# Gated linear attention with a gated convolution block: q, k and f packed into 12 of 16 columns, and one more convolution on VectorE

## The chip, the core and the metric

The kernel runs on one core of a Trainium2 chip. The metric is the device time of one execution in microseconds (us). The engines are named as in the profile: PE is TensorE's matmul (PEld its weight loads), DVE is VectorE, ACT is ScalarE, POOL is GpSimd, and SP is SyncE, whose queue issues nearly all transfers.

## The reference

```python
# B, H, S, D = 4, 8, 768, 48; five taps; d_model = H * D = 384; everything float32
f = 1 / (1 + exp(-f_logit))
for t in range(S):                                   # per batch and head, a 48 x 48 state
    state = f[t][:, None] * state + outer(k[t], v[t])
    y[t] = q[t] @ state
x = y.transpose(0, 2, 1, 3).reshape(B, S, H * D)
gate = sigmoid(sum(conv_w[j] * xp[:, j:j+S] for j in range(5)))  # xp: x with 4 zeros ahead, per channel
out = ((gate * (x @ w_val)) @ w_out)
```

## The kernel before

**Layout.** The sequence is cut into six chunks c of 128 positions (C). Two heads share a column: head 0 lies in rows 0 to 47, head 1 in rows 64 to 111, and rows 48 to 63 and 112 to 127 are pad rows. A column is a pair (batch b, pair of heads p), so there are BP = 16 columns of 128 positions, batch 3 being columns 12 to 15. q, k and v have two buffers each (`qb`, `kb`, `vb`), the decay logarithms three (`E1`, named e), beside `E2` (also e).

**Attention of a chunk.** `loadf`, `loadk`, `loadq`, `loadv` bring the operands in spans of columns. `pexp` and `pln` (ACT) make the decay logarithms. Their prefix sum over time is a matmul with the triangle `tri` for chunks 0 and 1 (`cum`, into PSUM banks `bk`) and a scan on DVE for chunks 2 to 5 (`scan`). `exp2` and `exp1` (ACT) take the exponentials with both signs, `pmulk` and `pmulq` (DVE) multiply them onto k and q in place. Per batch, `scores` or, from chunk 2, `scoresq` (PE, into `aps`), `mask` (DVE, into `asb`), `ktrans` (PE) and `kevac` (ACT), `dstate` (PE), `apply` or, for two batches at once, `applyq` (PE), `cross` and `crossb` (PE: q against the running state `ss`), and `xevac` (ACT, into `xf`). `stadd` (DVE) and `stmul` (ACT, eight pieces for one half of the columns) advance the state; `stmul` scales by the last column of `E1`.

**Projection.** The units n are 0 and 1 (chunk 0, two batches each), 2 to 5 (chunks 1 to 4), 6 and 7 (chunk 5, two batches each). `msplit` and `mlow` split x in a high and a low part. The convolution is either `conv n j` (PE, tap weights `wd`, five taps over three groups m of 128 channels: 60 matmuls for a chunk) for chunks below `CS`, or `mlast n m` (ACT) with four `mtap n m j` (DVE, in place in `gt`, for chunk 5 in `re`) from chunk `CS` on. Then `gate` (ACT), `mval` (PE, nine matmuls for each m), `mmul` (DVE), `mhigh` (ACT), `mrest` (DVE), `mout` (PE, nine matmuls), `mstore` (ACT and a transfer). `halo` hands the last four positions to the next chunk. In chunks below `CS` the channels lie rotated by 32-row groups (`TURN`), so that `wturn` makes rotated weights for the later chunks and one halo goes by transfers.

**Order.** `PROGRAM` is a text that lists every piece; each engine, and SP's queue, executes its instructions in just this order (class `Ordered`, line 129, is why nearly every row of the profile carries L129). What a piece waits for is kept by semaphores. `general` is a fallback that runs only when a flag at the end says that the fast way lost range.

Of the kernel before, what the change touches and what calls it, by code (L numbers as in the profile page):

```python
# [57 lines left out]
loadk 1 0; weight 0; loadq 1 0; scores 0 0; kevac 0 0; pmulk 0 2; loadf 2 0; exp1 0 2; dstate 0 0; mask 0 0;  # L58
exp2 0 1; ktrans 0 2; loadv 1 0; ktrans 0 3; exp1 0 1; pmulk 0 1; kevac 0 2; apply 0 0; weight 0; pexp 1 1; okc 0;
pmulq 0 1; ktrans 0 1; pmulq 0 2; xevac 0 0; scores 0 1; pln 1 1; weight 0; weight 0; weight 0; weight 0;  # L60
kevac 0 1; taps; cum 1 1; loadq 2 0; kevac 0 3; pexp 1 0; loadk 2 0; mask 0 1; pln 1 0; dstate 0 1; scores 0 2;
exp2 1 1; stadd 0 0; cum 1 0; exp1 1 1; mask 0 2; weight 2; weight 2; weight 2; apply 0 1; exp2 1 0;
weight 2; scores 0 3; weight 2; loadv 2 0; xevac 0 1; msplit 0; weight 2; dstate 0 2; loadq 2 1; exp1 1 0;
mask 0 3; weight 1; dstate 0 3; loadk 2 1; apply 0 2; weight 2; stadd 0 1; apply 0 3; weight 1; pmulk 1 0;
xevac 0 2; loadf 3 0; xevac 0 3; weight 1; ktrans 1 1; msplit 1; conv 0 0; weight 1; kevac 1 1; weight 1;
conv 0 1; pmulq 1 0; loadv 2 1; conv 0 2; pmulk 1 1; cross 1 0; pexp 2 0; weight 1; scores 1 0; okc 1; halo 1;
mlow 1; ktrans 1 0; conv 0 3; mask 1 0; weight 2; pln 2 0; conv 0 4; pmulq 1 1; scores 1 1; kevac 1 0; gate 0 2;
scan 2 0; dstate 1 1; loadk 3 0; dstate 1 0; apply 1 0; gate 0 0; mask 1 1; weight 4; gate 0 1; cross 1 1;
weight 1; ktrans 1 3; stadd 1 0; weight 4; wturn 0; scores 1 2; mlow 0; exp2 2 0; weight 4; apply 1 1;
weight 4; crossb 1 0; mask 1 2; weight 1; loadv 3 0; kevac 1 3; exp1 2 0; ktrans 1 2; loadq 3 0; pmulk 2 0;  # L70
dstate 1 3; scores 1 3; stmul 1 0; weight 4; apply 1 2; kevac 1 2; loadk 3 1; mask 1 3; weight 3; xevac 1 0;
pexp 3 0; dstate 1 2; wturn 1; weight 4; mval 0 2; stadd 1 1; scan 2 1; mval 1 1; weight 4; weight 3; mval 1 0;
pln 3 0; apply 1 3; mmul 0 2; weight 3; exp2 2 1; mval 0 1; weight 3; loadv 3 1; mmul 1 0; weight 3; exp1 2 1;
mval 0 0; weight 3; xevac 1 1; crossb 1 1; mmul 0 1; weight 3; pmulk 2 1; mval 1 2; xevac 1 2; loadq 3 1;
stmul 1 1; mmul 1 1; scan 3 1; ktrans 2 3; ktrans 2 2; kevac 2 3; ktrans 2 1; loadf 4 0; kevac 2 2; ktrans 2 0;
kevac 2 1; dstate 2 3; kevac 2 0; dstate 2 2; mmul 1 2; xevac 1 3; dstate 2 0; mmul 0 0; exp2 3 1; halo 2;
dstate 2 1; stadd 2 1; conv 2 0; pmulq 2 0; exp1 3 1; conv 2 1; stadd 2 0; msplit 2; scan 3 0; scoresq 2 1;
cross 2 0; pexp 4 0; conv 2 2; mask 2 1; weight 3; conv 2 3; exp2 3 0; mlow 2; scoresq 2 0; exp1 3 0; conv 2 4;
loadk 4 0; pln 4 0; mask 2 0; weight 4; mval 2 1; okc 3; pmulk 3 0; mhigh 1 0; mhigh 0 0; mhigh 0 2; mrest 1 0;
applyq 2 0; mhigh 1 2; mrest 0 2; mhigh 1 1; mrest 1 2; mhigh 0 1; mrest 1 1; gate 2 2; scan 4 1; loadq 4 0;  # L80
xevac 2 1; mout 1 1; loadv 4 0; stmul 2 0; mrest 0 1; mrest 0 0; mout 1 0; pmulq 2 1; mstore 1 1; gate 2 1; mout 0 2;
xevac 2 0; okc 2; pmulq 3 0; mstore 1 0; gate 2 0; scoresq 2 2; mstore 0 2; mmul 2 1; cross 2 1; pmulq 3 1; mout 0 1;
mask 2 2; mout 1 2; mstore 0 1; scan 4 0; scoresq 2 3; mstore 1 2; mout 0 0; loadk 4 1; mask 2 3; exp2 4 0; mval 2 0;
pmulk 3 1; exp2 4 1; scoresq 3 3; pmulk 4 0; applyq 2 1; mstore 0 0; mmul 2 0; exp1 4 1; pmulk 4 1; exp1 4 0;
ktrans 4 1; mhigh 2 1; okc 4; pmulq 4 0; loadv 4 1; stmul 2 1; loadq 4 1; ktrans 3 2; ktrans 4 0; mask 3 3;
xevac 2 3; ktrans 4 2; loadf 5 0; xevac 2 2; mval 2 2; mrest 2 1; mhigh 2 0; halo 3; kevac 3 2; mrest 2 0; mlast 3 1;
mlast 3 0; mtap 3 1 0; scoresq 3 0; msplit 3; mmul 2 2; dstate 3 2; mtap 3 0 0; ktrans 3 1; ktrans 3 3; kevac 4 2;
mask 3 0; ktrans 3 0; kevac 3 1; kevac 3 3; dstate 4 2; mtap 3 0 1; kevac 3 0; dstate 3 1; mhigh 2 2; dstate 3 3;
mtap 3 0 2; dstate 3 0; kevac 4 1; scoresq 3 1; stadd 3 1; pexp 5 0; mrest 2 2; ktrans 4 3; mtap 3 0 3; loadk 5 0;
mout 2 1; mask 3 1; kevac 4 3; mlast 3 2; mlow 3; kevac 4 0; pln 5 0; mout 2 2; mtap 3 2 0; mtap 3 2 1; gate 3 0;  # L90
mval 3 0; mtap 3 2 2; mtap 3 2 3; mstore 2 2; scan 5 1; gate 3 2; mout 2 0; mstore 2 1; mmul 3 0; exp2 5 1;
scoresq 4 1; scan 5 0; dstate 4 3; dstate 4 0; cross 3 0; exp1 5 1; applyq 3 0; stadd 3 0; mtap 3 1 1; exp2 5 0;
mtap 3 1 2; exp1 5 0; mtap 3 1 3; mval 3 2; loadq 5 0; mask 4 1; xevac 3 0; loadv 5 0; gate 3 1; pmulk 5 0;
scoresq 3 2; mmul 3 2; xevac 3 1; dstate 4 1; okc 5; mhigh 3 0; check; loadk 5 1; mval 3 1; mstore 2 0; mrest 3 0;
stmul 3 0; mask 3 2; mhigh 3 2; stadd 4 0; scoresq 4 0; mmul 3 1; cross 3 1; mrest 3 2; mhigh 3 1; applyq 3 1;
mask 4 0; mrest 3 1; pmulk 5 1; mout 3 2; xevac 3 3; loadv 5 1; pmulq 4 1; xevac 3 2; loadq 5 1; mlast 4 2; halo 4;
mlast 4 1; pmulq 5 0; mout 3 1; mlast 4 0; mtap 4 1 0; stmul 3 1; mtap 4 0 0; msplit 4; mtap 4 0 1; mout 3 0;
pmulq 5 1; mstore 3 1; mstore 3 2; mlow 4; scoresq 5 0; cross 4 0; mstore 3 0; stadd 4 1; applyq 4 0; mtap 4 1 1;
mtap 4 1 2; mtap 4 1 3; mval 4 0; stmul 4 0; mask 5 0; mtap 4 2 0; xevac 4 0; gate 4 1; mtap 4 2 1; cross 5 0;
xevac 4 1; mtap 4 2 2; scoresq 4 3; mtap 4 2 3; mval 4 2; mask 4 3; gate 4 2; mtap 4 0 2; mtap 4 0 3; scoresq 4 2;  # L100
mmul 4 2; gate 4 0; count; mval 4 1; mask 4 2; mhigh 4 2; mmul 4 0; mrest 4 2; mhigh 4 0; scoresq 5 3; mmul 4 1;
cross 4 1; mrest 4 0; mhigh 4 1; applyq 4 1; mrest 4 1; mout 4 1; stmul 4 1; mask 5 3; xevac 4 2; xevac 4 3;
mout 4 2; mlast 5 2; halo 5; msplit 5; mtap 5 2 0; mtap 5 2 1; mlast 5 1; cross 5 1; mlow 5; scoresq 5 2; mstore 4 1;
mlast 5 0; mout 4 0; mstore 4 2; mask 5 2; mtap 5 2 2; mtap 5 1 0; applyq 5 1; mstore 4 0; mtap 5 1 1; mtap 5 2 3;
mtap 5 1 2; gate 5 2; mval 5 1; mtap 5 1 3; xevac 5 2; xevac 5 3; mtap 5 0 0; gate 5 1; mlast 7 2; mtap 5 0 1;
msplit 7; mval 5 0; mtap 5 0 2; mlast 7 1; mmul 5 1; mlast 7 0; mtap 7 1 0; mhigh 5 1; mlow 7; mval 5 2; mtap 5 0 3;
mrest 5 1; gate 5 0; mtap 7 2 0; mval 7 0; mmul 5 0; mmul 5 2; mhigh 5 0; mval 7 2; mtap 7 2 1; mhigh 5 2; mrest 5 0;
scoresq 5 1; mrest 5 2; mval 7 1; mtap 7 2 2; mask 5 1; mout 5 2; mtap 7 2 3; mtap 7 0 0; gate 7 2; mtap 7 0 1;
mmul 7 2; mtap 7 0 2; mhigh 7 2; applyq 5 0; mtap 7 0 3; mstore 5 2; mrest 7 2; mtap 7 1 1; gate 7 0; mtap 7 1 2;
mmul 7 0; mtap 7 1 3; mhigh 7 0; mout 5 1; gate 7 1; mrest 7 0; xevac 5 1; mmul 7 1; xevac 5 0; mlast 6 2; mlast 6 1;  # L110
mtap 6 2 0; mlast 6 0; mtap 6 1 0; mout 5 0; mhigh 7 1; mtap 6 0 0; msplit 6; mtap 6 1 1; mrest 7 1; mstore 5 1;
mlow 6; mout 7 0; mtap 6 1 2; mstore 5 0; mtap 6 0 1; mval 6 2; mtap 6 0 2; mstore 7 0; mtap 6 0 3; mtap 6 1 3;
# [797 lines left out]
```

## Time and profile before

| | |
|---|---|
| median of 3 runs | 194.43 us (192.79 to 195.23) |
| profiled execution | 193.15 us |
| span of its profile | 191.5 us |
| granted TensorE clock | 0.995 |
| bytes moved | 32.64 MB, mean 170 GB/s |

The span is the time from the first to the last instruction; the profiled execution's own time is 1.65 us longer. In the rows, "out<-in" names the tiles, "x" counts instructions, "busy, mean ns" are the time that a group covers and the length of one instruction. Matmuls overlap, so the sum of their lengths is more than the time that they cover. A float32 matmul has two records.

### The profile page before, as it was taken

To read this page: it belongs to the slowest core of one execution; us is meant where nothing else is said; L and a number is where in the kernel's file an instruction comes from. 1 tells how busy PE (TensorE), PEld (TensorE's weight loads), DVE (VectorE), ACT (ScalarE), POOL (GpSimd) and SP (SyncE) were. 2 spreads that over 40 slices of the span, in tenths; PEclk is the share of its full clock that TensorE was granted. 3 is DMA by queue.
4 is the path that set the end of the run, shared out by engine and by line. 5 is a ranking of instruction groups with operands and counts; after the bars stand their busy time and mean duration, and the time that the engine had idled before them with its cause. 6 is when DMAs were issued, how large, how long until landed. Compare 5 with 4: busy or idle time off the path is not lost.

```text
span 191.5 us, 8303 instructions
## 1 busy us (share of the span) xinstructions
PE 180.2 (94%) x3706; PEld 144.8 (76%) x3706; DVE 162.2 (85%) x233; ACT 144.8 (76%) x284; POOL 13.7 (7%) x42
## 2 busy tenths in 40 slices
...
GB/s 194 344 419 416 416 415 409 415 349 245 203 114 285 41 113 62 206 128 135 350 48 104 113 12 266 130 183 156 15 3 3 3 167 3 3 54 4 140 87 65
DMA packets 12522, 32.64 MB, mean 170 GB/s; under 512 B 3008, under 2 KB 5440, under 8 KB 11456
## 3 DMA queue, kind: packets, MB, share of 16 engines
...
q10 hardware_dynamic: 432, 0.39, 0.7%
...
## 4 chain that ended last, share of the span: by engine, by line
PE 56%; DVE 19%; ACT 13%; issue 6%; DMA 3%; POOL 0%; ACTq 0%; DVEq 0%
PE bk L129 49%; PE aps L129 8%; DVE re L129 7%; DVE gt L129 5%; ACT ss L129 4%; DMA out<-osb 3%; ACT e L129 2%; ACT xf L129 2%; DVE asb L129 2%; DVE qb L129 1%; DVE rg L129 1%; DVE xL L129 1%; ACT osb L129 1%; DVE rqb L129 1%; ACT re L129 1%
## 5 line engine op out<-in xcount | busy, mean ns | idle before, releaser
L129 ACT ACTIVATE e<-e 112x512 f32<-112x512 f32 (+4 forms) x38 | 36.6, 997 | 4.1 <-DMA e<-in_ft 2.0
L129 PE MATMUL bk<-rg,woH 128*128 128x512 f32 (+1 forms) x108 | 30.1, 365 | 0.1
L129 DVE TENSOR_TENSOR asb<-aps,tri 128x768 f32<-128x768 f32 (+1 forms) x24 | 24.9, 1039 | 5.4 <-PE aps L129 4.0
L129 DVE SCALAR_TENSOR_TENSOR gt<-xf,cws,gt 128x512 f32<-128x512 f32 x36 | 26.5, 748 | 1.5 <-ACT gt L129 0.9
L129 PEld LDWEIGHTS aps<-qb,kb 48*64 48x64 f32 (+1 forms) x640 | 19.9, 144 | 7.3 <-issue 4.8
L129 PE MATMUL bk<-asb,vb 128*32 128x64 f32 (+2 forms) x1280 | 24.4, 232 | 0.4 <-issue 0.4
L129 PE MATMUL aps<-qb,kb 48*64 48x128 f32 (+2 forms) x640 | 23.7, 257 | 0.1
L129 PEld LDWEIGHTS bk<-asb,vb 128*32 128x32 f32 (+1 forms) x1280 | 20.0, 108 | 4.1 <-issue 1.1
L129 PEld LDWEIGHTS bk<-rg,woH 128*128 128x128 f32 x108 | 18.6, 188 | 4.3 <-issue 0.8
L129 DVE TENSOR_TENSOR kb<-kb,e 112x1024 f32<-112x1024 f32 (+1 forms) x13 | 14.8, 1137 | 6.0 <-DMA kb<-in_k 3.5
L129 PE MATMUL bk<-rg,woL 128*128 128x512 f32 (+1 forms) x54 | 19.4, 358 | 0.0
L129 ACT ACTIVATE ss<-u,e 112x48 f32<-112x48 f32 x64 | 15.3, 324 | 3.9 <-PE bk L129 3.9
L129 DVE TENSOR_TENSOR_SCAN e<-keep,e 112x1024 f32<-112x1024 bf16 x8 | 18.3, 2282 | 0.0
L129 PE MATMUL bk<-qb,ss 48*32 48x128 f32 x640 | 15.8, 275 | 1.5 <-ACT cb L129 1.2
L129 ACT COPY osb<-bk 128x512 f32<-128x512 f32 (+1 forms) x20 | 9.8, 495 | 9.1 <-DMA out<-osb 7.3
L129 DVE TENSOR_TENSOR qb<-qb,e 112x1024 f32<-112x1024 f32 (+1 forms) x13 | 14.8, 1146 | 0.0
L129 ACT COPY xf<-bk 128x384 f32<-128x384 f32 x24 | 10.8, 473 | 4.6 <-PE bk L129 4.6
L129 PEld LDWEIGHTS bk<-qb,ss 48*32 48x32 f32 x640 | 10.6, 106 | 4.6 <-issue 1.4
L129 PE MATMUL bk<-xH,wvH 128*128 128x256 f32 (+1 forms) x36 | 13.3, 370 | 0.4 <-ACT xf L129 0.4
L129 PE MATMUL bk<-xL,wvH 128*128 128x256 f32 (+1 forms) x36 | 12.2, 339 | 0.0
L129 PE MATMUL bk<-xH,wvL 128*128 128x256 f32 (+1 forms) x36 | 12.1, 337 | 0.0
L129 ACT CAST rg<-gt 128x512 fp32r<-128x512 f32 (+1 forms) x18 | 9.3, 546 | 3.7 <-DVE gt L129 3.7
...
## 6 DMA issues: line engine op xcount, KB each, us to landing
...
```

Of the source, the lines that this page charges most:

```text
L129: ins = emit(*a, **kw)
```

## The change

From chunk `DF = 1` on q, k and f hold 12 columns: batch 3's 48 rows of a head are laid out by the host in the pad rows of batches 0, 1 and 2 (16 rows each). `pexp`, `pln`, `cum`, `scan`, `exp1`, `exp2`, `pmulk` and `pmulq` then work on 128 rows and 12 columns, in spans of 8 and 4. After the multiplication new pieces `mvk`, `mvq` copy batch 3's rows by transfers on SP's queue into columns 12 to 15 (four transfers for the first span, two for the second), and `mve` does so for the last position of `E1` (six transfers), which `stmul` reads. `CS` goes from 2 to 1: chunk 1's convolution is done by `mlast` and `mtap`, its channels lie unrotated, its projection uses the rotated weights, and the halo by transfers is that of chunk 1. The order is written anew. The three tiles' unused rows are set once on POOL.

```diff
-CS = 2
+CS = 1
+DF = 1
+BD = BP - NP
+dense = lambda c, spans: [(a, min(b, BD)) for a, b in spans] if c >= DF else spans
+high = lambda c: 128 if c >= DF else 112
...
+    nc.gpsimd.memset(okc, 1.0)
...
+    for c in range(max(DF, 1), NB):
+        nc.gpsimd.memset(kw[c][32:64, BD:], 0.0)
+    for c in range(max(DF, 1), NE):
+        nc.gpsimd.memset(E1[c][32:64, BD + (2 if c == 2 else 0) :, C - 1 : C], 0.0)
...
     def scan(c, x0, x1):
-        fl = lambda t: t[:112, x0:x1].rearrange("p a t -> p (a t)")
+        fl = lambda t: t[: high(c), x0:x1].rearrange("p a t -> p (a t)")
...
     def pmul(t, e, c, x0, x1):
-        t = t[c % NB]
-        DVE.tensor_tensor(out=t[:, x0:x1], in0=t[:, x0:x1], in1=e[:112, x0:x1], op=ALU.mult)
+        t = t[c % NB][: high(c)]
+        DVE.tensor_tensor(out=t[:, x0:x1], in0=t[:, x0:x1], in1=e[: high(c), x0:x1], op=ALU.mult)
+    def move(t, x0, x1, cols=slice(0, C)):
+        for b in range(x0 // NP, x1 // NP):
+            for s in range(2):
+                SP.dma_start(t[s * 64 + 16 * b : s * 64 + 16 * b + 16, BD:, cols],
+                             t[s * 64 + D : s * 64 + 64, b * NP : (b + 1) * NP, cols])
...
+        "mvk": lambda c, n: move(kw[c % NB], *spans["s"](c)[n]), "mvq": lambda c, n: move(qw[c % NB], *spans["s"](c)[n]),
+        "mve": lambda c: move(E1[c % NE], 0, BD, slice(C - 1, C)),
...
     (host layout)
+        for b in range(B - 1):
+            for s in range(2):
+                y[DF:, s * 64 + D : s * 64 + 64, b * NP : (b + 1) * NP] = y[DF:, s * 64 + 16 * b : s * 64 + 16 * b + 16, BD:]
```

`PROGRAM` goes from 631 pieces to 665: five `conv 2 j` are gone, and three `mlast`, twelve `mtap`, ten `mvk`, ten `mvq` and four `mve` are new. Its start, and the stretch with the first moves of chunk 2:

```diff
-halo 0; loadf 0 0; loadf 0 1; loadq 0 0; loadv 0 0; loadk 0 0; loadk 0 1; loadk 0 2; wload 0; loadf 1 1; pexp 0 0;
-loadv 0 1; pln 0 0; busy 6; cum 0 0; loadq 0 1; pexp 0 2; loadq 0 2; loadf 1 0; pln 0 2; wload 1; exp2 0 0; busy 2;
-cum 0 2; exp1 0 0; pmulk 0 0; pexp 0 1; wload 2; pmulq 0 0; loadv 0 2; pln 0 1; ktrans 0 0; exp2 0 2; cum 0 1;
+halo 0; loadf 0 0; loadk 0 0; loadf 0 1; loadq 0 2; loadq 0 0; loadk 0 1; loadv 0 2; loadf 1 1; loadq 0 1; pexp 0 0;
+wload 0; pln 0 0; busy 6; cum 0 0; loadv 0 0; exp2 0 0; exp1 0 0; loadf 1 0; pmulk 0 0; pexp 0 1; loadv 0 1; busy 2;
+ktrans 0 0; pln 0 1; loadk 0 2; pexp 0 2; cum 0 1; pmulq 0 0; kevac 0 0; wload 2; pln 0 2; scores 0 0; wload 1;
+exp2 0 1; loadv 1 0; cum 0 2; exp1 0 1; loadk 1 0; pmulk 0 1; loadq 1 0; pexp 1 1; mask 0 0; pln 1 1; weight 0;
...
+mval 1 0; mvk 2 0; xevac 1 3; mval 1 1; weight 3; exp2 3 0; wturn 1; weight 3; scoresq 2 1; stmul 1 1;
+weight 3; mval 1 2; loadv 3 1; weight 3; mmul 0 1; mask 2 1; mval 0 2; weight 4; weight 3; loadf 4 0; mve 2;
+exp1 3 0; mmul 1 2; applyq 2 0; halo 2; mmul 0 2; msplit 2; okc 2; scan 3 1; mmul 1 1; exp2 3 1; mlow 2; scoresq 2 2;
+exp1 3 1; mvq 2 0; xevac 2 1; ktrans 2 1; xevac 2 0; ktrans 2 0; pmulq 3 1; kevac 2 1; mval 2 0; mve 3; mask 2 2;
+weight 3; pexp 4 0; mmul 1 0; pmulq 3 0; mhigh 1 2; dstate 2 1; mhigh 1 1; mvq 3 1; mhigh 0 0; scoresq 2 3;
...
```

More of the change, by code (lines that the diff above doesn't have):

```diff
@@ L58 @@
[L58 to L112, printed above, removed]
@@ new lines @@
+ktrans 0 0; pln 0 1; loadk 0 2; pexp 0 2; cum 0 1; pmulq 0 0; kevac 0 0; wload 2; pln 0 2; scores 0 0; wload 1;
+exp2 0 1; loadv 1 0; cum 0 2; exp1 0 1; loadk 1 0; pmulk 0 1; loadq 1 0; pexp 1 1; mask 0 0; pln 1 1; weight 0;
+ktrans 0 1; weight 0; pmulq 0 1; exp2 0 2; loadf 2 0; cum 1 1; weight 0; weight 0; weight 0; weight 0;
+taps; scores 0 1; kevac 0 1; pexp 1 0; dstate 0 1; mask 0 1; loadq 2 0; pln 1 0; dstate 0 0; loadk 2 0; apply 0 0;
+exp1 0 2; pmulk 0 2; apply 0 1; xevac 0 0; okc 0; stadd 0 0; ktrans 0 2; exp2 1 1; loadv 2 0; pmulq 0 2; cum 1 0;
@@ new lines @@
+xevac 0 1; kevac 0 2; msplit 0; exp1 1 1; mlow 0; scores 0 2; exp2 1 0; ktrans 0 3; mask 0 2; loadk 2 1; exp1 1 0;
+dstate 0 2; kevac 0 3; scores 0 3; okc 1; loadq 2 1; dstate 0 3; mask 0 3; weight 2; apply 0 2; weight 2;
+stadd 0 1; apply 0 3; xevac 0 2; weight 2; loadf 3 0; weight 2; xevac 0 3; msplit 1; pmulk 1 0; conv 0 0;
+loadv 2 1; pmulk 1 1; conv 0 1; mlow 1; ktrans 1 1; pmulq 1 0; ktrans 1 0; kevac 1 1; conv 0 2; kevac 1 0; mvk 1 1;
+weight 2; pexp 2 0; scores 1 0; weight 2; pmulq 1 1; cross 1 0; weight 2; mask 1 0; weight 1; dstate 1 1;
@@ new lines @@
+pln 2 0; mvq 1 1; dstate 1 0; conv 0 3; stadd 1 0; weight 1; scan 2 0; scores 1 1; apply 1 0; weight 1;
+ktrans 1 2; exp2 2 0; conv 0 4; weight 1; mvk 1 0; kevac 1 2; weight 1; exp1 2 0; dstate 1 2; weight 1;
+mvq 1 0; gate 0 1; mask 1 1; weight 2; scores 1 2; scan 2 1; halo 1; gate 0 0; apply 1 1; gate 0 2;
+pmulq 2 0; weight 1; crossb 1 0; loadk 3 0; exp2 2 1; mask 1 2; weight 4; loadv 3 0; cross 1 1; loadk 3 1;
+ktrans 1 3; loadq 3 0; pmulk 2 0; scores 1 3; wturn 0; stmul 1 0; pmulk 2 1; apply 1 2; mask 1 3; weight 1;
@@ new lines @@
+mvk 2 1; weight 4; scoresq 2 0; xevac 1 0; weight 4; xevac 1 1; cross 2 0; exp1 2 1; weight 4; kevac 1 3;
+apply 1 3; weight 4; pexp 3 0; pmulq 2 1; mval 0 0; weight 4; mvq 2 1; pln 3 0; mask 2 0; weight 3; mve 1;
+dstate 1 3; crossb 1 1; mmul 0 0; weight 3; stadd 1 1; mval 0 1; scan 3 0; xevac 1 2; weight 4; loadq 3 1;
+mval 1 0; mvk 2 0; xevac 1 3; mval 1 1; weight 3; exp2 3 0; wturn 1; weight 3; scoresq 2 1; stmul 1 1;
+weight 3; mval 1 2; loadv 3 1; weight 3; mmul 0 1; mask 2 1; mval 0 2; weight 4; weight 3; loadf 4 0; mve 2;
@@ new lines @@
+applyq 2 1; mtap 2 0 0; mlast 2 2; mvk 3 0; stadd 2 0; mtap 2 2 0; stmul 2 0; loadv 4 0; mtap 2 1 0; mout 0 2;
+mtap 2 0 1; loadq 4 1; xevac 2 3; mtap 2 0 2; xevac 2 2; mout 0 1; mstore 0 2; mtap 2 0 3; mtap 2 1 1; mout 1 0;
+gate 2 0; mtap 2 1 2; mout 1 2; mtap 2 1 3; mstore 0 1; mout 0 0; mmul 2 0; mstore 1 0; gate 2 1; mtap 2 2 1;
+mstore 1 2; scoresq 3 0; mmul 2 1; mstore 0 0; mout 1 1; mtap 2 2 2; mtap 2 2 3; mval 2 2; mstore 1 1; mask 3 0;
+gate 2 2; mhigh 2 1; halo 3; scan 4 0; mhigh 2 0; ktrans 3 0; msplit 3; ktrans 3 1; scoresq 3 1; mmul 2 2;
@@ new lines @@
+ktrans 2 3; kevac 3 0; loadk 5 0; mask 3 1; ktrans 2 2; kevac 3 1; dstate 3 0; kevac 2 3; loadk 4 1; kevac 2 2;
+mlow 3; dstate 3 1; mhigh 2 2; dstate 2 3; dstate 2 2; exp2 4 0; cross 3 0; loadv 4 1; mrest 2 2; mval 3 0;
+mrest 2 0; mrest 2 1; mlast 3 0; stadd 2 1; mlast 3 2; stadd 3 0; mout 2 1; mtap 3 0 0; stmul 2 1; pmulk 4 0;
+mout 2 0; mtap 3 0 1; exp1 4 0; mvk 4 0; mtap 3 0 2; mstore 2 1; mtap 3 0 3; mlast 3 1; loadf 5 0; mout 2 2;
+pmulq 4 0; mstore 2 0; gate 3 0; mtap 3 1 0; mvq 4 0; mtap 3 1 1; scoresq 4 1; mstore 2 2; mtap 3 1 2; applyq 3 0;
@@ new lines @@
+mmul 3 0; pexp 5 0; mtap 3 1 3; pmulk 3 1; mtap 3 2 0; mval 3 2; mvk 3 1; mask 4 1; loadq 5 0; gate 3 1; loadv 5 0;
+mtap 3 2 1; scoresq 3 2; mtap 3 2 2; xevac 3 1; mtap 3 2 3; ktrans 3 2; xevac 3 0; ktrans 3 3; stmul 3 0; mask 3 2;
+loadk 5 1; mval 3 1; scan 4 1; gate 3 2; okc 3; kevac 3 3; cross 4 0; mmul 3 2; kevac 3 2; dstate 3 3; mhigh 3 0;
+mmul 3 1; dstate 3 2; mhigh 3 2; mrest 3 0; scoresq 3 3; mhigh 3 1; stadd 3 1; cross 3 1; exp2 4 1; mrest 3 1;
+ktrans 4 0; mask 3 3; ktrans 4 1; scoresq 4 0; mrest 3 2; kevac 4 1; pmulk 4 1; kevac 4 0; dstate 4 1; exp1 4 1;
@@ new lines @@
+mask 4 0; dstate 4 0; mvk 4 1; pln 5 0; applyq 3 1; mve 4; stadd 4 0; pmulq 4 1; scan 5 0; mvq 4 1; mout 3 1;
+xevac 3 2; xevac 3 3; loadq 5 1; msplit 4; loadv 5 1; scan 5 1; scoresq 4 2; halo 4; okc 4; exp2 5 0; mlow 4;
+mout 3 0; exp1 5 0; mask 4 2; mstore 3 1; mlast 4 2; pmulq 5 0; mval 4 1; stmul 3 1; mtap 4 2 0; mvq 5 0; mtap 4 2 1;
+scoresq 4 3; mlast 4 0; mtap 4 2 2; mlast 4 1; cross 4 1; mtap 4 2 3; mstore 3 0; applyq 4 0; mtap 4 1 0; exp2 5 1;
+mtap 4 1 1; exp1 5 1; gate 4 2; mask 4 3; mval 4 2; okc 5; mtap 4 1 2; xevac 4 1; pmulq 5 1; xevac 4 0; check;
@@ new lines @@
+mvq 5 1; stmul 4 0; mval 4 0; mmul 4 2; pmulk 5 1; mtap 4 0 0; mvk 5 1; applyq 4 1; mtap 4 1 3; mtap 4 0 1; gate 4 1;
+mtap 4 0 2; mmul 4 1; ktrans 4 3; mtap 4 0 3; xevac 4 3; ktrans 4 2; xevac 4 2; count; cross 5 0; pmulk 5 0;
+kevac 4 3; kevac 4 2; scoresq 5 2; gate 4 0; halo 5; mvk 5 0; msplit 5; dstate 4 2; mmul 4 0; dstate 4 3; mask 5 2;
+mout 3 2; mlow 5; scoresq 5 0; stadd 4 1; mstore 3 2; mval 5 1; mhigh 4 1; mask 5 0; mhigh 4 2; mhigh 4 0; mrest 4 1;
+stmul 4 1; mrest 4 0; scoresq 5 1; mrest 4 2; mval 5 0; mask 5 1; mlast 5 2; mlast 5 1; mtap 5 2 0; mlast 5 0;
```

75 lines of the change are left out of this document (49 added, 26 removed).

## The prediction

> **What bounds the kernel now.** I read the page's busy line first, then busy time by stage, then the chain of work that ended last, and last the order of instructions on TensorE and VectorE.
>
> ```profile
> PE 180.2 (94%) x3706; PEld 144.8 (76%) x3706; DVE 162.2 (85%) x233; ACT 144.8 (76%) x284; POOL 13.7 (7%) x42
> ```
>
> ```profile
> 0.00:14.00 14.00, 11.03 (x84) 8.69 (x84) 7.38 (x17) 10.42 (x20) 3.45 (x16) 1.00 0.88 315
> 14.00:184.00 170.00, 166.28 (x3600) 133.35 (x3600) 154.86 (x218) 133.21 (x262) 10.29 (x26) 1.00 0.46 162
> 184.00:191.50 7.50, 2.92 (x25) 2.72 (x23) 0.00 (x0) 1.12 (x3) 0.00 (x0) 0.88 0.32 97
> ```
>
> The columns of the stages are PE, PEld, DVE, ACT and POOL busy, the granted clock (1.00, so no throttle to win back), the DMA share and GB/s. From 14 to 184 us PE has 3.7 us without work in 170, DVE 15.1. PE leads, DVE is second.
>
> ```profile
> 120.33 9.49 PE bk L129 x212
> 155.50 2.09 DVE gt L129 x3
> 168.19 0.80 DVE re L129 x2
> 183.58 3.35 PE bk L129 x26
> ```
>
> ```profile
> 159.67 0.40 PE L129 MATMUL bk<-xL,wvH 128*128 128x512 f32 x1
> 159.91 0.39 PE L129 MATMUL bk<-xH,wvL 128*128 128x512 f32 x1
> 160.14 0.40 PE L129 MATMUL bk<-xH,wvHt 128*128 128x512 f32 x1
> ```
>
> The chain (start, length, what) runs on PE up to about 150 us and then mostly on DVE, and returns to PE at 183.58. But the matmuls beside that DVE stretch start 0.24 us apart without a hole, each counted as about 0.40 because it overlaps the next. So both engines are full there: whatever shortens PE helps only as far as DVE finishes earlier too. That is the main doubt of this prediction.
>
> The Trainium skill, "Perfetto Trace Analysis", section "Identifying the Most-Contended Engine", calls matmul busy time a poor measure and wants the weight-load share instead. By it PE stands at 76% and DVE's 85% leads, and a change that hands DVE work off PE should bring nothing: the first rival below. The even starts speak against it here, so I keep PE as the bound.
>
> **The change part by part.** The convolution of chunk 1 leaves PE (60 matmuls, 120 in the records), and the prefix sum of chunk 1 shrinks from 16 columns to 12.
>
> ```profile
> 60.90:69.30 8.40, 5.56 (x120) 1.61 (x120) 0.00 (x0) 1.00 0.34 94
> ```
>
> ```profile
> 16.79 2.00 PE L129 MATMUL bk<-tri,xf 128*112 128x128 f32 x16
> ```
>
> The first row is the busy time of the tile wd alone, PE's 5.56 us of convolution. The second is eight columns, so four are 1.0 us; that saving falls into the start and is counted there. **PE: -5.56 us.** On DVE and ACT, by groups (busy, mean ns):
>
> ```profile
> L129 DVE SCALAR_TENSOR_TENSOR gt<-xf,cws,gt 128x512 f32<-128x512 f32 x36 | 26.5, 748 | 1.5 <-ACT gt L129 0.9
> L129 DVE TENSOR_TENSOR_SCAN e<-keep,e 112x1024 f32<-112x1024 bf16 x8 | 18.3, 2282 | 0.0
> L129 DVE TENSOR_TENSOR qb<-qb,e 112x1024 f32<-112x1024 f32 x11 | 13.5, 1230 | 0.0
> L129 DVE TENSOR_TENSOR qb<-qb,e 112x512 f32<-112x512 f32 x2 | 1.4, 683 | 0.0
> L129 ACT ACTIVATE e<-e 112x2048 f32<-112x2048 f32 x8 | 15.3, 1911 | 1.8 <-DMA e<-in_f 1.8
> L129 ACT ACTIVATE e<-e 112x1024 f32<-112x1024 f32 x8 | 8.4, 1057 | 0.2
> L129 ACT ACTIVATE e<-e 112x512 f32<-112x512 f32 x16 | 9.1, 621 | 0.0
> L129 ACT ACTIVATE gt<-xf,cws 128x512 f32<-128x512 f32 x9 | 6.2, 720 | 0.1
> ```
>
> DVE gains 12 taps x 26.5/36 = 8.8 us. It loses half of every second multiplication: ten (k and q, chunks 1 to 5) x (1230 - 683) = 5.5 us; and half of every second scan. No scan of 512 is in the trace: it lies between nothing saved and half, 1.14; I take 1.1, since the multiplications nearly halve: 4 x 1.1 = 4.4. **DVE: 8.8 - 5.5 - 4.4 = -1.1 us**, that is, as full as before. ACT drops about a quarter of e: 8 x 0.45 of the long pair (2048 to 1536 elements), 4 x 0.44 of exp1, 8 x 0.25 of exp2, some 1.5 in chunk 1, together 8.9, against 3 x 0.72 of new starts: -6.7 us. ACT isn't the bound from 14 us on (133.21 of 170), so this counts nothing. Loads of q, k and f lose a quarter; the waits they caused on ACT (1.8 us) had PE work beside them, so nothing, at most 1.8. The memsets on POOL lie in the first microseconds, where the triangle is finished well ahead of the first prefix sum; nothing, at most their own length.
>
> **The start** is reordered, and here I walk through the new order with the old durations.
>
> ```profile
> 5.39 0.95 ACT L129 ACTIVATE e<-e 128x896 f32<-128x896 f32 x1 [0.54 <-DMA e<-in_ft]
> 7.44 1.09 ACT L129 ACTIVATE e<-bk 112x512 f32<-112x512 f32 x2
> 11.51 1.16 PE L129 MATMUL aps<-qb,kb 48*128 48x128 f32 x16
> 12.78 1.23 DVE L129 TENSOR_TENSOR asb<-aps,tri 128x1024 f32<-128x1024 f32 x1 [0.58 <-PE aps L129]
> 14.15 1.08 PE L129 MATMUL bk<-asb,vb 128*32 128x128 f32 x32
> 15.29 0.48 ACT L129 COPY xf<-bk 128x384 f32<-128x384 f32 x1
> 27.52 0.82 PE L129 MATMUL bk<-ident,kb 112*128 112x112 f32 x4 [0.23 <-ACT xf L129]
> 28.28 3.22 PE L129 MATMUL bk<-xf,wd 32*32 32x512 f32 x72
> 33.33 0.60 PE L129 MATMUL bk<-ident,kb 112*128 112x112 f32 x4
> ```
>
> Before, ACT used the wait for the first prefix sum (up to 7.44) for the logits of batches 2 and 3 (the row at 5.39). Now they stand behind exp2, exp1 and batch 1. From 7.44 on ACT has, back to back: four exponentials of 512 for batches 0 and 1 (0.55 each), the small logits of batch 1 (1.35), the large ones of batches 2 and 3 (2.1), two evacuations of k (0.95), chunk 1's logits (1.4 and 2.3), and exp2 and exp1 of batches 2 and 3 (2.2): 12.5 us, so to about 20. (The pieces that no row here shows are estimates by their columns from the row at 5.39, with 0.2 for each sum that is read out.) The q multiplication (1.2), then scores 0 2 (from 22 at the latest, behind the prefix sum of chunk 1), mask, scores 0 3, mask, apply 0 3 and its evacuation follow one another: 22 + 1.16 + 1.23 + 1.16 + 1.23 + 1.08 + 0.48 = 28.3, and with queueing 28.6. That is where the convolution of chunk 0 can begin. Before it began at 28.28, with one transpose group of chunk 1 (0.60) already behind it. PE is then 0.9 us behind, though it has 1.0 less of prefix sum to do; I take **+1.0 us**, with bounds of -0.5 (the two idle holes fill) and +2.5 (each of the two masks waits one piece of DVE more).
>
> **The moves.** 84 transfers between SBUF rows join SP's queue: six per chunk for k, six for q, six for the last column of e (not in chunk 5).
>
> ```profile
> L129 SPq DMA_DIRECT2D xf<-xf x5: 616/679/1555, 60.4 to 64.1; - x5
> DMA to landing us min/median/max: 1.8/3.5/6.8
> xf<-xf SPq DMA_DIRECT2D x2, 4.0 KB, 2.3
> SPq L129 <- ACT osb L129: 56.4, 16, 14.5
> ```
>
> ```profile
> 56.56 1.68 ACT ss L129 x7
> 92.00 2.37 PE bk L129 x9
> 94.37 0.83 PE aps L129 x32
> 71.46 1.87 PE L129 MATMUL bk<-asb,vb 64*32 64x64 f32 x128
> 73.14 1.22 PE L129 MATMUL bk<-qb,ss 48*32 48x128 f32 x32
> ```
>
> The only small SBUF-to-SBUF transfers of the trace take 0.68 us of SP each and land 1.8 to 6.8 us after issue (the landing row covers the loads into xf too). SP works in order and is held for up to 14.5 us by one wait. What a late move delays is batch 3's scores, k transposes and cross products, and everything on PE behind them. Most moves have more than 5 us of PE work ahead of their use. The tightest is scoresq 2 3: SP must pass loadf 4 0 (which waits until stmul 1 1 has read the buffer), the six of mve 2 and the four of mvq 2 0: 0.33 + 9 x 0.68 + 2.3 of landing = 8.8 us after stmul 1 1. PE has in that time two halves of 2.37, 1.87 + 1.22, 0.83, two transposes of 0.60 and one 2.37, 9.9 us, of which stmul itself (eight pieces, 1.9) takes the first part: 8.0. It is 0.8 us late; with 3.5 of landing it is 2.0. Scores 1 3 (moved while the loads still run) and ktrans 3 3 (behind mvk 3 1) are just covered. I take **+1.0 us**, with bounds of 0 and +5.
>
> The Trainium skill, "DMA: Bandwidth & Descriptors", "Rules for kernel authors", says that transfers under 64 KB pay mostly overhead and should be joined; its fit gives 2.1 us for a 32 KB move. That speaks against 84 pieces. With that figure, an estimate, scoresq 2 3 would be 0.6 us late and not 0.8. The landing rows above are mostly longer than the fit.
>
> **Sum**: -5.56 + 1.0 + 1.0 = -3.6 us on the profiled execution of 193.15 us (span 191.5): 189.6. The median of the runs, 194.43, lies 0.66% above that execution, so 190.9. About 2%, 3.9 us, is what a measurement of this kernel can tell from no change; the forecast lies just within.
>
> **The rivals.** *DVE becomes the bound.*
>
> ```profile
> 182.55 0.98 DVE L129 TENSOR_TENSOR rqb<-re,rkb 128x256 fp32r<-128x256 f32 x2
> ```
>
> Today DVE ends at 183.5, 8.0 us before the span's end, and idles 14.6 of the 169.5 us before that. In the new order four output groups (each about half of 2.37, 1.2) stand behind the last subtraction, not three, so DVE must end 9.2 before the end. If it keeps its 14.6 us of idle, the span is 14 + 154.86 - 1.1 + 14.6 + 9.2 = 191.6 and nothing is gained: 194.5. The forecast needs DVE to lose 4.7 us of idle. For it: each tap chain now waits for the last use of gt. Against it: much of that idle was waiting for PE.
>
> *Everything is covered*: the order loses nothing at the start and no move is late. Then 5.56 + 1.0 go: 186.6, as a median 187.8. For it: PE's holes of 3.7 us that the new order could also fill; against it: the walk above.
>
> *The moves are late* (slower). Scores 1 3, scoresq 2 3 and ktrans 3 3 each meet a landing of 6.8 in place of 2.3: 3 x 4.5 = 13.5 us on top of 189.6 without the 1.0 for partial cover, 202 at most; with two of three 197.6, as a median 198.9. It decides from 4.6 us of lateness in sum (5.56 less 1.0), 1.5 us at each of the three. For it: SP's order and the maximum landing; against it: the long landings fall into the stage in which the loads fill the queues.
>
> **How the numbers follow.** Forecast 0.50 (about 189 to 193, a third of it over 2% faster), DVE 0.20 (193 to 195), everything covered 0.20, late moves 0.10. Faster by over 2%: 0.17 + 0.20 and a little of the rest, 0.40. Slower by over 2%: most of the last, 0.08. Within: 0.52. The range goes from below the covered case, 186.5, to above the DVE case, 195.5; outside it are late moves and a little of the covered case.
>
> **What would show it.** PE busy falls to about 174, DVE stays near 161, ACT falls to about 138. The first convolution matmul starts between 28 and 30 us. Waits of PE (or its weight loads) on transfers into qb or kb add up to about 1 us; over 4 and the last rival holds. If DVE's idle from 14 us to its last instruction is still over 13 us with PE idle beside it, the first rival holds. The prediction is wrong if the instruction order alone changed PE's holes by more than the 3.7 us that it had.

## Result and profile after

The changed kernel takes 206.91 us (median of 4 runs, 206.22 to 207.32) against 193.61 for the kernel before: ratio 1.068, 95% interval 1.058 to 1.078. It is slower by 13 us, where 190.9 was forecast. Ratios below leave out disturbed executions; medians hold all, so the two can differ, by up to 2%.

The page of the changed kernel (its profiled execution 206.66 us, span 204.9): busy time by engine, the granted clock in 40 slices, and the chain that ended last.

```profile
PE 180.5 (88%) x3578; PEld 146.3 (71%) x3578; DVE 160.5 (78%) x245; ACT 140.3 (68%) x287; POOL 14.6 (7%) x46
PEclk9999999996699966589999999999999999999999
PE 51%; DMA 28%; ACT 7%; SPq 7%; issue 3%; DVE 2%; ACTq 0%
```

DVE and ACT came out close to the prediction's sums (161 and 138). PE's instructions are fewer, but its busy time has not fallen: the clock row shows why, for it drops to 5 and 6 tenths in two places. The chain, which was PE, DVE and ACT before, is now 28% DMA and 7% SP's queue (SPq); more than half of that DMA share lies in the first 41 us, where the chain runs through the first loads, so the page alone doesn't tell where the time went. Busy time by stage (columns PE, PEld, DVE, ACT, POOL, granted clock, DMA share, GB/s):

```profile
0.00:40.00 40.00, 33.87 (x596) 25.38 (x596) 29.77 (x48) 27.97 (x53) 6.04 (x23) 1.00 0.93 347
40.00:65.00 25.00, 22.13 (x458) 18.54 (x449) 20.85 (x27) 17.47 (x35) 5.85 (x7) 0.86 0.39 106
65.00:95.00 30.00, 21.13 (x464) 16.47 (x460) 17.82 (x28) 18.32 (x39) 1.69 (x4) 0.77 0.47 136
95.00:190.00 95.00, 92.55 (x1994) 75.28 (x1993) 86.49 (x132) 71.03 (x147) 1.07 (x12) 1.00 0.30 95
```

From 65 to 95 us no engine is full: PE 21 of 30 us at a clock of 0.77, DVE 18, ACT 18. Something outside the engines holds them all. The timelines show it: first ScalarE's two long waits of that stretch, then SP's queue beside them (start, length, what).

```profile
66.03 1.01 ACT L138 ACTIVATE ss<-u,e 112x48 f32<-112x48 f32 x4 [3.75 <-DMA e<-e]
77.69 1.48 ACT L138 ACTIVATE e<-e 128x1536 f32<-128x1536 f32 x1 [5.36 <-DMA e<-in_f]
```

```profile
59.50 5.25 SPq L138 DMA_DIRECT2D e<-e  x6
64.86 0.53 SPq L138 DMA_DIRECT2D qb<-in_q  x1
65.43 3.65 SPq L138 DMA_DIRECT2D kb<-kb  x4
69.18 2.45 SPq L138 DMA_DIRECT2D wvLt<-wvL  x4
71.67 0.60 SPq L138 DMA_DIRECT2D vb<-in_v  x1
72.36 0.39 SPq L138 DMA_DIRECT2D e<-in_f  x1
72.80 3.92 SPq L138 DMA_DIRECT2D e<-e  x6
76.76 2.72 SPq L138 DMA_DIRECT2D qb<-qb  x4
```

`loadf 4 0` (e<-in_f) may start once `stmul 1 1` (the row at 66.03) has read its buffer, at 67.04. SP issues it at 72.36, because it is still issuing `mvk 2 0`, four transfers of `wturn` and a load, one after the other with hardly a gap. ScalarE therefore waits 5.36 us for the logits. The six transfers of `mve 2` and the four of `mvq 2 0` stand behind that load, so they are late as well. TensorE stands four times:

```profile
46.85 0.64 PE L138 MATMUL bk<-qb,ss 48*32 48x128 f32 x24 [1.55 <-DMA qb<-qb]
69.98 0.49 PE L138 MATMUL bk<-xH,wvH 128*128 128x512 f32 x1 [1.19 <-ACT xH L138]
71.77 0.80 PE L138 MATMUL bk<-xL,wvH 128*128 128x512 f32 x1 [1.30 <-DVE xL L138]
80.35 2.29 PE L138 MATMUL aps<-qb,kb 48*64 48x128 f32 x32 [4.57 <-DVE rg L138]
```

All four holes go back to moved data that came late. The first ends with a moved row of q. The second and third go back to ScalarE's wait for the moved column of e (the row at 66.03), behind which it makes xH. The fourth, the largest, the profile puts down to DVE's rg. But `scoresq 2 3` stands in the order ahead of the `mrest` pieces that write rg then, so it doesn't wait for them. By the semaphores in the trace TensorE's wait for `mvq 2 0` ends at 80.29 us: of its four transfers the third lands at 80.26, and the last, at 80.86, holds TensorE for 0.35 us more.

In the clock records, half clock begins at 47.55 (for 6.83 us), 71.44 (3.41) and 78.27 (10.24), in or just behind these holes: 20.5 us in all, of which the kernel before had none between 9 and 189 us. What one transfer takes of SP (ns: smallest, median, largest; then first and last start):

```profile
L138 SPq DMA_DIRECT2D kb<-kb x30: 507/580/1782, 31.6 to 158.7; - x30
L138 SPq DMA_DIRECT2D qb<-qb x30: 507/587/1707, 34.7 to 147.9; - x30
L138 SPq DMA_DIRECT2D e<-e x24: 585/596/1363, 59.5 to 136.7; - x24
L138 SPq DMA_DIRECT2D kb<-in_k x12: 327/398/1572, 1.3 to 123.0; - x12
```

So 84 x 0.59, about 49 us (54 us when their lengths are added up), of a queue that works strictly in order; a transfer of 0.2 KB (e) costs it as much as one of 32 KB (kb, qb).

### The profile page after: what moved, and what is told of

Read it like the earlier page. It is cut to its first block, busy times and chain, and to the rows that moved or that the text cites. A ratio compares the mean times of both kernels' runs of the same rounds, so it can differ in the third digit from the quotient of the medians.

```text
span 204.9 us, 8193 instructions
## 1 busy us (share of the span) xinstructions
PE 180.5 (88%) x3578; PEld 146.3 (71%) x3578; DVE 160.5 (78%) x245; ACT 140.3 (68%) x287; POOL 14.6 (7%) x46
## 4 chain that ended last, share of the span: by engine, by line
PE 51%; DMA 28%; ACT 7%; SPq 7%; issue 3%; DVE 2%; ACTq 0%
PE bk L138 45%; DMA qb<-in_q 15%; SPq L138 7%; PE aps L138 6%; DMA vb<-in_v 6%; DMA e<-in_f 5%; ACT e L138 2%; ACT ss L138 1%; DVE rg L138 1%; DMA qb<-qb 1%; DMA e<-e 1%; ACT xf L138 1%; ACT xH L138 1%; DVE gt L138 1%; ACT L138 1%
## 5 line engine op out<-in xcount | busy, mean ns | idle before, releaser
L138 ACT ACTIVATE e<-e 128x512 f32<-128x512 f32 (+5 forms) x38 | 30.1, 818 | 10.9 <-DMA e<-in_f 6.5
L138 DVE SCALAR_TENSOR_TENSOR gt<-xf,cws,gt 128x512 f32<-128x512 f32 x48 | 34.8, 747 | 0.7
L138 PE MATMUL aps<-qb,kb 48*64 48x64 f32 (+2 forms) x640 | 26.9, 273 | 6.3 <-DVE rg L138 4.6
L138 PEld LDWEIGHTS aps<-qb,kb 48*64 48x64 f32 (+1 forms) x640 | 22.6, 156 | 13.5 <-DVE rg L138 5.0
L138 DVE TENSOR_TENSOR gt<-bk,gt 128x512 f32<-128x512 f32 (+1 forms) x18 | 10.6, 593 | 7.2 <-ACT gt L138 3.8
L138 DVE TENSOR_TENSOR kb<-kb,e 128x1024 f32<-128x1024 f32 (+3 forms) x13 | 11.9, 930 | 3.3 <-ACT e L138 3.3
L138 DVE TENSOR_TENSOR_SCAN e<-keep,e 128x1024 f32<-128x1024 bf16 (+1 forms) x8 | 14.3, 1793 | 0.0
L138 DVE TENSOR_TENSOR qb<-qb,e 128x1024 f32<-128x1024 f32 (+3 forms) x13 | 12.3, 949 | 2.3 <-ACT ksb L138 2.3
L138 DVE TENSOR_TENSOR rg<-gt,rg 128x512 fp32r<-128x512 f32 (+1 forms) x18 | 10.1, 595 | 4.8 <-ACT rg L138 4.7
L138 PE MATMUL bk<-xH,wvH 128*128 128x256 f32 (+1 forms) x30 | 11.4, 380 | 1.2 <-ACT xH L138 1.2
```

The lines of the kernel that those rows point to most:

```text
L138: ins = emit(*a, **kw)
```

## Experiments

**Is it the transfers?** *e2_no_moves* leaves them out and sets columns 12 to 15 once on POOL; batch 3 is computed from other data.

```diff
     def move(t, x0, x1, cols=slice(0, C)):
+        return
```

> The changed kernel with the packed columns, but the moves left out: columns 12 to 15 hold what was set once or what stood there, so batch 3 is computed from other data; every instruction on PE, VectorE and ScalarE is there. Theory: 186 to 192 us, no half clock before the end, PE idle from 40 to 100 us falls from 12 us to under 4. Rival (order or taps): over 203 us. A third reading (the packed spans themselves are slow): e1 fast, this one slow.

Measured: 189.86 us, ratio 0.980 (0.972 to 0.987). So the transfers cost 17.0 us (206.91 - 189.86), and the rest of the change gains about 2%. Its page and stages:

```profile
PE 175.5 (92%) x3578; PEld 143.6 (76%) x3578; DVE 160.1 (84%) x245; ACT 140.5 (74%) x287; POOL 14.7 (8%) x47
PEclk9999999999999999999999999999999999999999
```

```profile
0.00:40.00 40.00, 34.51 (x508) 27.09 (x520) 25.30 (x44) 26.54 (x49) 6.10 (x24) 1.00 0.93 342
40.00:65.00 25.00, 22.51 (x510) 17.95 (x486) 24.65 (x30) 21.77 (x46) 5.40 (x7) 1.00 0.47 142
65.00:95.00 30.00, 29.30 (x720) 25.08 (x720) 29.08 (x43) 25.50 (x52) 2.24 (x6) 1.00 0.42 139
```

PE's busy time by its clock, this kernel against the changed one: 22.5 and 22.13 x 0.86 = 19.0 from 40 to 65 us; 29.3 and 21.13 x 0.77 = 16.3 from 65 to 95 us. So 3.5 and 13.0 us of PE's work are lost there. Of these 16.5 us, 8.6 are idle time (22.5 - 22.1 and 29.3 - 21.1), and 8.0 are the slower clock (22.13 x 0.14 and 21.13 x 0.23). The stretch up to 40 us can't be compared like this: the profiled execution of e2, 191.64 us, had lost over 4 us at its start (first convolution matmul at 32.9 us, against 28.6 in the changed kernel).

**Is it the time that they take of SP, or their data being late?** *e11_idle_transfers* has them all, between spare rows.

```diff
-                SP.dma_start(t[s * 64 + 16 * b : s * 64 + 16 * b + 16, BD:, cols], t[s * 64 + D : s * 64 + 64, b * NP : (b + 1) * NP, cols])
+                SP.dma_start(spare[i : i + 16, :, cols], spare[0:16, :, cols])    # i: 16 to 112 in turn
```

> The changed kernel in its own order with the 84 transfers at their places and in their sizes, but between spare rows: they wait for no product and nobody waits for them. Batch 3 is computed from other data, as in the kernel without transfers (189.9). Theory of SP's time (about 0.55 us each, in order, ahead of loadf 4 0 and the other loads): most of the 17 us is there, 197 to 206, with ACT waiting for loadf 4 0 by 3 us or more. Rival, the waits of the transfers for products and of PE for transfers are what costs: 189 to 192.

Measured: 206.36 us, ratio 1.065 (1.059 to 1.071): all of the loss, although no transfer waits for a product and nobody waits for a transfer. What they take of SP, and the waits (total, times, longest):

```profile
L138 SPq DMA_DIRECT2D spare<-spare x84: 507/588/2001, 31.5 to 149.2; - x84
```

```profile
ACT e L138 <- DMA e<-in_f: 10.8, 1, 10.8
ACT osb L138 <- DMA out<-osb: 10.2, 3, 8.7
PE bk L138 <- DMA wvLt<-wvL: 4.7, 1, 4.7
```

What is late is what stands behind them in the queue: the logits of a later chunk, the stores that free `osb`, the rotated weights. SP's time is enough to cause the whole loss. Who waits changes with the kernel: in the changed kernel the moved rows are what TensorE waits for first, here, where nobody needs them, it is the loads, stores and weights behind them.

**Does the number count, or the bytes?** *e10_joined*: the host lays row 3r+b into pad row r of batch b, so that one transfer for each head moves all three batches; 28 instead of 84. Here `loadk 5 0` overwrites part of chunk 3's pad rows before they are moved, so batch 3 of chunk 3 is computed from other data; *e12_joined_whole* moves that k batch by batch (32 transfers) and changes nothing of the computation.

```diff
-        for b in range(x0 // NP, x1 // NP):
-            for s in range(2):
-                SP.dma_start(t[s * 64 + 16 * b : s * 64 + 16 * b + 16, BD:, cols], t[s * 64 + D : s * 64 + 64, b * NP : (b + 1) * NP, cols])
+        ...                                       # returns at the first of the two pieces
+        for s in range(2):                        # at the later of the two pieces
+            SP.dma_start(t[s * 64 : s * 64 + D, BD:, cols], t[s * 64 + D : s * 64 + 64, :BD, cols])
+        # e12, k of chunk 3, by batch: t[s * 64 + b : s * 64 + D : 3, BD:, cols] <- t[s * 64 + D : s * 64 + 64, b * NP : (b + 1) * NP, cols]
```

> The changed kernel with its transfers joined: the host lays row 3r+b of a head of batch 3 into pad row r of batch b, so that one transfer per head moves all three batches, at the place of the later of the two pieces; 28 transfers in place of 84, the same bytes. Theory of the number of transfers on SP's queue: two thirds of the 46 us of SP time go, and with them most of the 17 us that the moves cost: 191 to 196. Rival, the chain of product, transfer and use is what is late: the first span now waits for the second product, and 96 KB land later than 32: 204 to 212.

> The joined kernel with the k of chunk 3 moved batch by batch (four and two transfers), because loadk 5 0 stands between its two pieces; 32 transfers, nothing left out or changed in the computation. Theory of the number of transfers on SP's queue: four more than 28 at 0.6 us in a stretch where SP waits anyway, so as the joined one: 191.5 to 194. Rival, something in the joined run was cheap only because a load overtook a transfer: 196 or more.

Measured: 192.84 us, ratio 0.992 (0.988 to 0.996), and 192.39, ratio 0.985 (0.980 to 0.990). The same bytes in a third of the transfers bring back 14 of the 17 us. The number of transfers is what costs, not the bytes. (SP itself also waits longer for loads to land, into kb, qb, vb and e 20.2 us in the changed kernel against 5.5 in e2; how the 17 us divide between issuing and these waits no run shows.) In e13 below, which has the same transfers, a transfer of 96 KB takes SP no longer than one of 32 KB did: 

```profile
L138 SPq DMA_DIRECT2D qb<-qb x10: 566/580/628, 35.6 to 132.0; - x10
```

**Does another queue do?** *e3_moves_pool*: all 84 on POOL's queue.

```diff
-                SP.dma_start(
+                POOL.dma_start(
```

> The changed kernel with all 84 moves issued from POOL's queue in place of SP's. Theory that SP's queue is what is late: SP is free for the loads, the load of f for chunk 4 is issued some 5 us sooner, 190 to 198 us, unless POOL's own waits on PE hold the moves. Rival that a move's own landing time is what is late, whoever issues it: stays at 205 to 208 us.

Measured: 198.34 us, ratio 1.009 (1.004 to 1.014), just above the range of the first theory. Half of the loss goes by the medians, two thirds by the ratios (1.068, 1.009, and 0.980 without transfers). But POOL works in order too: it waits for products, and SP then waits for POOL's transfers before it may load over their rows:

```profile
POOL kb L138 <- DVE kb L138: 16.0, 5, 5.3
```

```profile
SPq L138 <- DMA kb<-kb: 8.7, 2, 6.1
SPq L138 <- DMA qb<-qb: 8.1, 1, 8.1
```

**Is the halved clock the cause?** *e4_fill* puts 37 idle matmuls into the holes (7 before `cross 1 1`, 10 before `mval 2 0`, 20 before `scoresq 2 3`).

```diff
+    def fill(n):
+        for _ in range(n):
+            PE.matmul(free[0][:], idle[:, 0:128], idle[:], start=True, stop=True)
... fill 7; cross 1 1; ... fill 10; mval 2 0; ... fill 20; scoresq 2 3;
```

> The changed kernel with 37 empty matmuls (7, 10 and 20, each 0.21 us at full clock) put into PE's three largest holes (before cross 1 1, mval 2 0 and scoresq 2 3). They do no work that is used. If the holes cause the half clock: the stretches at half clock (20.5 us in all before the end) shrink to under 7, and the time falls by 4 to 9 us, to 198 to 203. If the half clock has another cause, or the holes' length alone counts: 206 to 210 us, the clock as before.

Measured: 209.63 us, ratio 1.087 (1.079 to 1.095); the expected gain is a miss. Half clock before the end fell from 20.5 to 10.2 us, and ScalarE waited as before, in sum even longer:

```profile
67.97 1.01 ACT L138 ACTIVATE ss<-u,e 112x48 f32<-112x48 f32 x4 [8.04 <-DMA e<-e]
78.25 1.48 ACT L138 ACTIVATE e<-e 128x1536 f32<-128x1536 f32 x1 [3.98 <-DMA e<-in_f]
```

SP issued `loadf 4 0` at 73.10, against 72.36. So less halved clock beside an unchanged queue brought nothing back: the wait moved. The 37 matmuls take time of PE as well, so this run doesn't tell what the halved clock costs by itself.

**The two halves of the change.** *e1_no_dense* (the changed kernel unpacked and without transfers) settled nothing. Its time is the one that its rival expected, but for a reason of its own: the new order loads columns 12 to 15 of `kb` ahead of batch 3's last use, so PE waits for that load once for 13.2 us, and batch 3 is computed from other data.

```diff
-DF = 1
+DF = NC
...
     def move(t, x0, x1, cols=slice(0, C)):
+        return
```

> The new order and the convolution of chunk 1 on VectorE, but q, k and f in all 16 columns again and no moves. Theory (the moves fill SP's queue, so that moved rows and loads come late, and PE's holes lower its clock): SP has 84 transfers fewer, the holes at 45, 70 and 76 us and the half-clock stretches vanish, 188 to 195 us, although VectorE and ScalarE have some 10 and 9 us more to do. Rival (the new order itself, or the taps on VectorE, cost the time): stays over 203 us.

Measured: 216.41 us, ratio 1.116 (1.105 to 1.127). *e5_conv_only* therefore starts from the kernel before:

```diff
-CS = 2
+CS = 1
-... conv 2 0 ... conv 2 4 ... gate 2 m
+... mlast 2 m; mtap 2 m 0; mtap 2 m 1; mtap 2 m 2; mtap 2 m 3; gate 2 m
```

> The kernel before with one part of the change alone: the convolution of chunk 1 is done by mlast, mtap and the unrotated channels, at the places where its conv stood in the old order; nothing is packed and nothing is moved. PE loses 5.56 us of matmuls, VectorE gains 12 taps, 8.8 us (162 to 171). If PE is the bound: 193.2 less 5.6, and up to 2 for chains that wait for the taps: 187.5 to 190. Rival, VectorE is as full: no gain or a loss, 192 to 198. Nothing is added to the queue of SyncE, so the theory of that queue expects no halved clock.

Measured: 203.16 us, ratio 1.050 (1.045 to 1.054): slower than both of its expectations, where PE as the only bound had asked for 187.5 to 190. The clock was halved for 20.5 us too, which was not expected, since nothing was added to SP's queue. Its busy line, then stages, first this kernel, then the kernel before, and holes of PE in this kernel:

```profile
PE 180.6 (90%) x3586; PEld 147.5 (73%) x3586; DVE 170.8 (85%) x245; ACT 146.6 (73%) x287; POOL 13.6 (7%) x42
```

```profile
62.00:92.00 30.00, 21.46 (x380) 17.78 (x358) 28.49 (x34) 19.38 (x38) 3.10 (x5) 0.71 0.24 76
```

```profile
62.00:92.00 30.00, 28.82 (x740) 21.38 (x721) 28.19 (x31) 25.08 (x52) 3.20 (x6) 1.00 0.44 127
```

```profile
64.39 1.51 PE L128 MATMUL aps<-qb,kb 48*64 48x128 f32 x32 [2.02 <-DVE asb L128]
77.15 0.38 PE L128 MATMUL bk<-rg,woH 128*128 128x256 f32 x1 [1.45 <-DVE rg L128]
88.98 1.56 PE L128 MATMUL aps<-qb,kb 48*64 48x128 f32 x32 [2.44 <-DVE asb L128]
```

VectorE was already full there (28.2 of 30). With 9 us more, PE waits for it, in the three holes shown for 5.9 us, and is busy for 21.5 of 30 at a clock of 0.71. VectorE is a second bound. In this order the convolution can't leave PE unless something relieves VectorE, as packing does: 170.8 us busy here, 160.1 in e2. Whether another order could hide the taps without packing was not tried. *e6_dense_old_order* is the packing alone, its transfers right behind each product:

```diff
 CS = 2
+DF = 1
+pmulk c n; mvk c n   ...   pmulq c n; mvq c n   ...   exp1 c 0; exp1 c 1; mve c
```

> The other part alone: packed columns and all 84 transfers, each right behind its multiplication or exponential in the OLD order, and chunk 1's convolution on PE as before. Theory of SP's queue (84 transfers at 0.55 us hold up loads and one another): slower than before in any order, 197 to 205, with PE waiting for transfers in all by 8 us or more. Rival, the new order is at fault (transfers, loads and weights of the first 95 us crowded together): about as before, 191 to 195.

Measured: 223.58 us, ratio 1.152 (1.145 to 1.159), worse than expected. PE waits for moved rows and a load, ScalarE for stores:

```profile
ACT osb L135 <- DMA out<-osb: 10.5, 2, 6.0
PE bk L135 <- DMA qb<-qb: 5.8, 1, 5.8
PE bk L135 <- DMA vb<-in_v: 5.0, 1, 5.0
PE bk L135 <- DMA kb<-kb: 2.9, 1, 2.9
```

So the transfers cost more in the old order than in the new, and the new order without them (e2) is faster than the kernel before: the new order isn't at fault.

**Versions with most of the loss gone.** *e13_joined_e_on_act*: as e12, the eight transfers of the last column of e issued by ScalarE, which wrote it.

```diff
-        "mve": lambda c: move(E1[c % NE], 0, BD, slice(C - 1, C)),
+        "mve": lambda c: move(E1[c % NE], 0, BD, slice(C - 1, C), queue=ACT),
```

> The same, and the eight transfers of the last column of e are issued by ScalarE, which has just written that column, and not by SP. SP loses 8 x 0.6 = 4.8 us of queue between 49 and 66 us and a wait for exp1. Theory of SP's queue: nearer to the kernel without transfers (189.9): 190 to 192. Rival, ScalarE's own queue is as tight (0.6 us for each ahead of the next exponential): 192.5 to 196.

Measured: 191.70 us, ratio 0.983 (0.978 to 0.988).

```profile
PE 174.8 (92%) x3578; PEld 142.3 (75%) x3578; DVE 160.3 (84%) x245; ACT 139.6 (73%) x287; POOL 14.9 (8%) x46
```

```profile
65.00:95.00 30.00, 27.92 (x540) 23.65 (x533) 26.90 (x39) 23.68 (x50) 1.70 (x4) 1.00 0.50 151
```

PE is back at 27.9 of 30 us and at full clock in the stage that had been lost. Its step beyond e12 (192.39, overlapping intervals) is not resolved. *e14_joined_old_start* takes the first 85 pieces in the old order:

```diff
-halo 0; loadf 0 0; loadk 0 0; loadf 0 1; loadq 0 2; loadq 0 0; ...
+halo 0; loadf 0 0; loadf 0 1; loadq 0 0; loadv 0 0; loadk 0 0; ...    (to apply 0 1, then the rest as it was)
```

> The same as e13, with the first 85 pieces in the order of before and the rest as in the changed kernel. PE was busy 52.7 us of the first 60 in the joined run against 54.9 in before. If the new start is what keeps the joined kernel from its 190: 188 to 190.5. Rival, work that PE does earlier at the start waits later for products of VectorE, which is full from 30 us on: within 1 us of e13.

Measured: 192.00 us, ratio 0.990 (0.986 to 0.994), its rival's answer: the old start gains nothing. *e16_joined_bank_first* goes after one hole of e13 and the halved clock behind it:

```diff
-exp1 5 1; gate 4 2; mask 4 3; mval 4 2; okc 5; mtap 4 1 2; xevac 4 1;
+exp1 5 1; xevac 4 1; gate 4 2; mask 4 3; mval 4 2; okc 5; mtap 4 1 2;
```

> The joined kernel with e on ScalarE, and one piece moved in the order: xevac 4 1 (the copy that frees a PSUM bank) stands ahead of gate 4 2 and its table load on ScalarE, not behind. In e13 PE has a hole of 1.6 us at 129.9 us that ends as that copy ends (131.2), and the clock is then halved for 3.41 us, which costs about 1.7. Theory that holes of PE cost twice, once as idle time and again as a halved clock: both go, 188.5 to 190.5, and no halved clock between 12 us and 188 us. Rival, PE waits for something else there, or the gate that is now later opens the same hole at the next product: 191 to 193, with a halved clock at 130 to 136 us as in e13.

Measured: 193.02 us, ratio 0.985 (0.977 to 0.993): no gain. The hole at 130 us and its half clock did go, but the profiled execution has another, at a place where e13's had one of 0.53 us:

```profile
53.30 0.71 PE L138 MATMUL bk<-asb,vb 128*32 128x128 f32 x17 [2.46 <-issue]
```

with 3.41 us of half clock from 54.12. Whether that hole is the price of the moved piece or changes from execution to execution, one profile can't say. The joined kernels stand at 191.7 to 193.0 us; by their ratios they are 0.8 to 1.7% faster than the kernel before. Each interval is below 1, but the gains are under the 2% that the prediction named as what a measurement of this kernel can tell.

## Why the prediction was wrong, by its steps

**The moves, +1.0 (0 to +5): this is the step that failed.** They cost 17.0. The price of a transfer was nearly right (0.68 us assumed, 0.59 measured), and the place called the tightest, `scoresq 2 3`, is where the largest hole lies. From the issue of `loadf 4 0` to the last landing of `mvq 2 0` it took 8.5 us (72.36 to 80.86), and 8.8 were forecast. What failed is the start of that count: it took SP as free when `stmul 1 1` ends (67.04), and SP was 5.3 us behind, still issuing the rest of `mvk 2 0`, four transfers of `wturn` and a load. So scores came over 4 us late, not 0.8. The step looked at each move by itself; it did not add some 49 us to SP's queue. Three more waits were put at nothing: `cross 1 1` for q (1.55 us), `stmul 1 1` for the moved column of e (3.75 us of ScalarE, then holes of 1.19 and 1.30 on PE), and the logits, loads, weights and stores behind the moves. e11 shows that these last cost as much when nobody needs the moved rows.

**The rival of late moves** had the right sign. Its sign to look for, over 4 us of PE's waits for transfers into qb and kb, came true: 1.55 and 4.57 us in two holes, though the profile names only the first. Its price was wrong: it priced three landings of 6.8 us, at most 202 in all. The third transfer of `mvq 2 0` landed 2.0 us after its issue (78.27 to 80.26); it was issued late.

**The clock.** "1.00, so no throttle to win back" did not ask whether one could be lost. The trace of before has no halved clock between its start and its end, so nothing in it could price this; every kernel above that is slower than the kernel before shows it. In the changed kernel the holes come first, and the halved clock makes up about half of what PE lost between 40 and 95 us, 8.0 of 16.5 us.

**The convolution (-5.56) and the start (+1.0).** Without the moves the sum was 193.15 - 5.56 + 1.0 = 188.6, as a median 189.8; e2 gave 189.86. As a ratio, 0.976 forecast and 0.980 measured (0.972 to 0.987), this agrees; that the medians agree to 0.1 us is luck, since the kernel before had a median of 193.2 beside e2 and not 194.43. The start fits in the changed kernel (first convolution matmul at 28.6 us, forecast 28 to 30, 28.3 before), but not in every execution: 32.9 in e2's. PE's busy time fell by 4.7 us in e2 (180.2 to 175.5) and 5.4 in e13 (174.8), where about 6 was forecast. That it is 180.5 in the changed kernel goes with the halved clock.

**VectorE** was rightly called as full as before (160.5 for 161). As a rival bound it did not come true in this change, though its sign did: from 14 us to its last instruction VectorE is idle for 28.5 us in the changed kernel, with PE idle for 15.1, because both wait; in e2 it is 12.5 and 5.6. The rival's sum has a slip: the forecast needed VectorE to lose 3.6 us of idle time, not 4.7, because the 1.1 us of less work was already in it. e5 shows how near this bound is: take the packing away, keep the old order, and the same convolution makes the kernel 9.5 us slower.
